# A new order table for a fused attention and two-MoE kernel, and the last four stores on ScalarE's queue

## The chip, the cores and the metric

One core of one Trainium2 chip runs the whole kernel. The metric is the device time of one execution in microseconds (us); lower is better. TensorE (PE) does the matrix products, VectorE (DVE), ScalarE (ACT) and GpSimd (POOL) the work between them, and SyncE (SP) issues nearly all transfers.

## What is computed

Three stages, one after the other. First a gated linear attention over 4 batches, 8 heads, 768 steps and a head size of 48; its result, transposed, is x with 3072 rows and 384 columns. Then a feed-forward layer of width 2048 with a rational function in the middle, and a second one of width 1536 with a gate:

```python
for t in range(S):
    state = alpha[:, :, t, :, None] * state + np.einsum('bhd,bhe->bhde', k[:, :, t], v[:, :, t])
    y[:, :, t] = np.einsum('bhd,bhde->bhe', q[:, :, t], state)
...
h = x @ w_in
P = a[0] + a[1] * h + a[2] * h**2 + a[3] * h**3
Q = 1.0 + np.abs(b[0]) * np.abs(h) + np.abs(b[1]) * h**2
x = (P / (Q + 1e-06)) @ w_out
...
g = x @ w_gate
out = (g * (1.0 / (1.0 + np.exp(-g))) * (x @ w_val)) @ w_out2
```

The weights arrive as 64-bit floats.

## The kernel before, in words

**Precision.** TensorE works on 32-bit numbers rounded to a shorter form, so each operand is kept as a high part and a low part (the rest), and each product is three matmuls: high by high, high by low, low by high (`mm3`, L954 to L957 in moe1; L1209 to L1211 for the last product of moe2). The low part is a subtraction, on GpSimd or on VectorE: `low` (L643, the instruction's line is L645) for weights, `sub` (L923, line L925) for x and for gg, the result of the rational function.

**Attention** (L749). The 3072 steps are cut in 24 chunks of 128. For a chunk, TensorE transposes alpha, k and q (aT, kT, qT, L770), ScalarE copies alpha (al, L779), VectorE runs two scans along the steps, which give running products (bb, L786) and the same backwards (cc, L794), with a reciprocal between them (L790); ScalarE takes the last product of each head (bC, L798). VectorE scales k and q with them (kt L802, qt L812), TensorE makes the scores (sc, L821), which ScalarE copies (aa, L830) and GpSimd masks (L835); then come a transpose back (kn_ps L846, kn L849), the values and the update of the state (upd L865, yT L870 and L876), the state itself (st_c L899, L902, L904; st_s L909) and the store of the chunk's x (L890).

**Weights.** `split_` (from L616) turns a 64-bit tile into high and low parts: a load (L639), two VectorE instructions that cut and join bits (e L669, x L675), and for the first six tiles three more on VectorE (r L683 and L689, x L693), for the others one on ScalarE and one of GpSimd (L697, L702); ScalarE writes the high part (L680, L699) and `low` the low part. The first feed-forward has 16 tiles of w_in (win) and 16 of w_out (wout).

**First feed-forward** (moe1, L959). x comes in six blocks of 512 rows. `load_x` (L929) loads three tiles of a block (xr, L938) and makes their high and low parts (L943, L925). For each of 16 tiles of the width, TensorE makes h (nine matmuls), the three other engines the rational function (t1, t2, t4, L988 to L1010, h L1003 and L1006), and ScalarE and GpSimd the two parts of gg (L1014, L925); TensorE adds gg times wout into three accumulators (acc). At the end of a part the accumulators are evicted (ys, L1039, L1040, L1045) and stored. The blocks are worked on in parts that are interleaved with attention: h of the first tile of block 0 is the first MoE matmul of the program, and block 1's h follows when its x is there.

**Second feed-forward** (moe2, L1150). From about 545 us on nothing but this is left for TensorE: gate and value products, the gate's function, and the last product, which in the last blocks lands with rows on partitions (po, L1209 to L1211). Each of the last block's four row tiles is evicted by ScalarE (L1273) or VectorE (L1274) into os and stored (L1279). In the last block (n == NT // TB - 1) the odd row tiles' stores are issued by ScalarE, the even ones by SyncE; all other stores are SyncE's (L1278).

**What sets the order.** The functions above only enter operations in a plan: `Plan.op` (L250) keeps, for each, its possible forms (engine, cost, function) and what it depends on. `ORDER` (L21), a table of 3746 numbers found by a search, says in which order they are emitted: a number is 2 x operation + choice of form, so that 1325 is operation 662 in its second form. `Plan.order` (L276) walks the table, asserts that what an operation depends on has been emitted, and gives out PSUM banks and weight tiles, first free first. Each engine runs its instructions in the table's order, and semaphores keep the dependencies; a wait on an engine holds up all that is behind it there. For most operations the form is fixed; for `low`, `sub` for x, the step t2 of the rational function (L988 on ScalarE, or GpSimd) and evictions the table chooses the engine. The first forms of `low` are VectorE for the first six weight tiles and GpSimd after them; the last bit of an entry is the choice.

```python
for x in table:
    i, k = x >> 1, x & 1
    _, how, deps, writes, follows = self.ops[i]
    assert i not in done and done.issuperset(deps) and done.issuperset(follows)
```

Of the kernel before, what the change touches and what calls it, by code (L numbers as in the profile page):

```python
# [457 lines left out]
def gla_moe_moe2_kernel(  # L458
# [15 lines left out]
    nc = tc.nc  # L474
    ctx.enter_context(tc.manual_schedule())
    B, H, S, D = q.shape
    NT, DM = out.shape
# [8 lines left out]
    TB = 512  # L486
# [82 lines left out]
    for nm in "akqv":  # L569
        for i in range(NBV if nm == "v" else 1):  # L570
            t = A.tile([128, H, 64], F32, name=f"nat{nm}{i}")
# [760 lines left out]
    t, vs2 = end_a + 5.14, []  # L1332
# [61 lines left out]
```

## Time and profile before

| what | value |
|---|---|
| time, median of 3 runs | 988.67 us (988.14 to 989.16) |
| the profiled execution: its time / its span | 987.1 us / 985.3 us |
| busy, share of the span: TensorE | 969.0 us (98%) |
| VectorE, ScalarE, GpSimd | 80%, 60%, 46% |
| matmuls (PE instructions) | 5355 |
| transfers | 113.51 MB, mean 115 GB/s |

The profiled execution's span is measured on the chip; 1.8 us of its time lie around the span. A matmul record overlaps the next one (512 columns follow each other every 0.23 us and are shown with 0.39), so a busy TensorE is not one at its peak. In rows of a timeline the first number is the start in us, the second the duration in us; "x3" means that three instructions of a kind are joined, and the brackets give the idle time of the engine before it and what ended that. Names as `t<-t,h` are the tiles written and read.

### The profile page before, as it was taken

What the parts mean: (1) busy time and instruction counts of PE and PEld (TensorE: products, weight loads), DVE (VectorE), ACT (ScalarE), POOL (GpSimd) and SP (SyncE); (2) the same over time, 40 slices, a digit from 0 to 9 for tenths busy, and PEclk for the clock granted to TensorE, in tenths of its full rate; (3) what the DMA queues carried; (4) which work ended last, traced back from release to release, by engine and by line L of the source; (5) the groups of instructions that cost most, each with busy time, mean ns of one, the idle gap of its engine ahead of it and who ended that gap; (6) DMA issues with size and microseconds to landing.
All of it is one profiled execution on the core that took longest, in us unless ns stands there. A gap on an engine that the chain in (4) does not pass through costs nothing.

```text
span 985.3 us, 15291 instructions
## 1 busy us (share of the span) xinstructions
PE 969.0 (98%) x5355; PEld 805.6 (82%) x5355; DVE 786.9 (80%) x1493; ACT 588.9 (60%) x1078; POOL 450.5 (46%) x426
## 2 busy tenths in 40 slices
PE   8899999999999999999999999999999999999997
PEld 7777888888888888888888888888888888888886
DVE  7999999999889888888898896799887767733222
ACT  4588998899999787789988675222122222212111
POOL 3368888799877676777987555000000000000000
PEclk9999999999999999999999999999999999999999
DMA  8978666531223242101221663346665545501000
GB/s 184 208 186 220 150 156 152 157 103 37 57 88 94 54 140 70 55 25 53 91 86 45 218 188 127 113 129 196 176 179 187 165 140 150 161 1 33 1 0 34
DMA packets 167137, 113.51 MB, mean 115 GB/s; under 512 B 115472, under 2 KB 140560, under 8 KB 167056
## 3 DMA queue, kind: packets, MB, share of 16 engines
q1 hardware_dynamic: 166768, 112.10, 40.7%
q8 instruction: 43, 0.70, 0.3%
q10 hardware_dynamic: 288, 0.39, 0.1%
q14 instruction: 38, 0.31, 0.1%
HBM read 95.95 MB, written 16.52 MB: 114 GB/s over the span
## 4 chain that ended last, share of the span: by engine, by line
PE 84%; DVE 8%; ACT 4%; issue 2%; POOL 1%; DMA 1%; SPq 0%; DVEq 0%; ACTq 0%; POOLq 0%
PE acc L955 6%; PE acc L956 6%; PE acc L957 6%; PE h L955 5%; PE h L957 5%; PE h L956 5%; PE pg L957 5%; PE pg L955 5%; PE pg L956 5%; PE pv L957 5%; PE pv L955 5%; PE pv L956 5%; PE po L955 4%; PE po L957 4%; PE po L956 4%
## 5 line engine op out<-in xcount | busy, mean ns | idle before, releaser
L925 POOL TENSOR_TENSOR gg<-t,gg 128x512 fp32r<-128x512 f32 x96 | 129.8, 1352 | 52.2 <-ACT gg L1014 50.9
L998 POOL TENSOR_TENSOR t<-t,t 128x512 f32<-128x512 f32 x96 | 127.7, 1332 | 29.2 <-ACT t L988 20.6
L1177 DVE TENSOR_TENSOR sg<-sg,pv 128x512 f32<-128x512 f32 (+1 forms) x73 | 49.4, 678 | 101.3 <-PE pv L957 101.0
L1179 ACT CAST pp<-sg 128x512 fp32r<-128x512 f32 (+1 forms) x73 | 44.8, 615 | 142.1 <-DVE sg L1177 126.7
L1175 ACT ACTIVATE sg<-pg 128x512 f32<-128x512 f32 (+1 forms) x73 | 43.0, 591 | 144.0 <-PE pg L957 143.8
L955 PE MATMUL h<-xt,win 128*128 128x512 f32 x288 | 114.4, 397 | 0.2 <-DVE wo_x L675 0.2
L955 PE MATMUL acc<-gg,wout 128*128 128x512 f32 x288 | 113.9, 396 | 0.5 <-DVE win_x L675 0.5
L957 PE MATMUL h<-xt,win 128*128 128x512 f32 x288 | 112.4, 390 | 0.0
L957 PE MATMUL acc<-gg,wout 128*128 128x512 f32 x288 | 112.3, 390 | 0.0
L956 PE MATMUL acc<-gg,wout 128*128 128x512 f32 x288 | 112.3, 390 | 0.0
L956 PE MATMUL h<-xt,win 128*128 128x512 f32 x288 | 112.2, 390 | 0.0
L957 PE MATMUL pg<-yy,wg 128*128 128x512 f32 x216 | 84.2, 390 | 0.0
L956 PE MATMUL pg<-yy,wg 128*128 128x512 f32 x216 | 84.2, 390 | 0.0
L955 PE MATMUL pg<-yy,wg 128*128 128x512 f32 x216 | 84.1, 389 | 0.0
L957 PE MATMUL pv<-yy,wv 128*128 128x512 f32 x216 | 84.0, 389 | 0.0
L956 PE MATMUL pv<-yy,wv 128*128 128x512 f32 x216 | 84.0, 389 | 0.0
L955 PE MATMUL pv<-yy,wv 128*128 128x512 f32 x216 | 84.0, 389 | 0.0
L1004 DVE SCALAR_TENSOR_TENSOR t<-t,h 128x512 f32<-128x512 f32 x96 | 65.4, 682 | 19.2 <-ACT h L1003 18.7
L995 ACT ACTIVATE t<-h,prm 128x512 f32<-128x512 f32 x96 | 73.8, 775 | 7.1 <-POOL gg L925 6.7
L1102 DVE TENSOR_SCALAR_CACHE_REDUCE chk_x<-chk_e 128x384 f32<-128x384 uint32 x136 | 73.6, 549 | 2.7
L1002 ACT ACTIVATE t<-t,oneps 128x512 f32<-128x512 f32 x96 | 69.5, 724 | 9.3 <-POOL t L998 8.9
L999 DVE TENSOR_TENSOR t<-t,h 128x512 f32<-128x512 f32 x96 | 65.1, 680 | 10.2 <-ACT t L995 10.0
(154 smaller groups left out, 2472.8 us busy)
## 6 DMA issues: line engine op xcount, KB each, us to landing
chk<-in_moe_w_out_dram SPq DMA_DIRECT2D x28, 384.0 KB, 3.2
yr<-y1d SPq DMA_DIRECT2D x36, 256.0 KB, 2.9
xr<-xd SPq DMA_DIRECT2D x27, 256.0 KB, 3.4
y1d<-ys SPq DMA_DIRECT2D x27, 256.0 KB, 3.2
win_st<-in_moe_w_in_dram SPq DMA_DIRECT2D x16, 384.0 KB, 4.1
wout_st<-in_moe_w_out_dram SPq DMA_DIRECT2D x16, 384.0 KB, 3.9
chk<-in_moe_w_in_dram SPq DMA_DIRECT2D x16, 384.0 KB, 3.5
nata<-in_alpha_dram SPq DMA_DIRECT2D x24, 192.0 KB, 3.6
```

The costliest lines, as they stand in the source:

```text
L925: return lambda: eng.tensor_tensor(out_(), in0(), in1().bitcast(F32), ALU.subtract)
L955: nc.tensor.matmul(out_, wh, xh, start=start, stop=False)
L956: nc.tensor.matmul(out_, wh, xl, start=False, stop=False)
L957: nc.tensor.matmul(out_, wl, xh, start=False, stop=stop)
L995: plan.op(v, [act(T, lambda: nc.scalar.activation(t4(), h(), AF.Identity, scale=a3, bias=a2), 2, False)], (hb,), (b4,))
L998: plan.op(v, [pool(T, lambda: nc.gpsimd.tensor_tensor(t1(), t1(), t2(), ALU.mult))], (b1, b2), (b1,))
L999: plan.op(v, [dve(T, lambda: nc.vector.tensor_tensor(t4(), t4(), h(), ALU.mult))], (b4, hb), (b4,))
L1002: plan.op(v, [act(T, lambda: nc.scalar.activation(t2(), t1(), AF.Ln, bias=oneps), 1)], (b1,), (b2,))
L1004: plan.op(v, [dve(T, lambda: nc.vector.scalar_tensor_tensor(t1(), t1(), ONE_EPS, h(), ALU.add, ALU.mult))], (b1, hb), (b1,))
L1102: [(DVE, 0.5, lambda: nc.vector.tensor_scalar(dst(), src(), bound, 0.0, op_, ALU.add, accum_out=cnt.t[:, c : c + 1]))],
L1177: plan.op(v, [(DVE, 0.07 + 0.53 * d, lambda sg=sg, z=z: nc.vector.tensor_tensor(sg.t[:, z], sg.t[:, z], pv.t[:, z], ALU.mult))], (sg, pv), ...
L1179: plan.op(v, [(ACT, 0.1 + 0.43 * d, lambda sg=sg, pp=pp, z=z: nc.scalar.copy(pp.t[:, 0, z], sg.t[:, z]))], (sg,), (pp,))
```

## The change

Three edits. In the table, 2791 of the 3746 entries differ: those from the second to number 2895 (with few exceptions), and four at the end. Operations and their dependencies are the same. On the engines' own sequences, TensorE's 551 operations differ at 221 places, VectorE has 1331 operations instead of 1333, ScalarE 1064 instead of 1076 and GpSimd 423 instead of 409; SyncE's transfers differ at 208 of 377 places. One hundred operations change their engine: 17 weight subtractions go from GpSimd to VectorE and 17 the other way, 28 of t2 from ScalarE to GpSimd and 18 back, 7 subtractions for x from GpSimd to VectorE and 3 back, 5 evictions of the first feed-forward from ScalarE to VectorE and 4 back, and the eviction of the last row tile of the last block from ScalarE to VectorE. The third edit is the queue of the last block's stores: all four on ScalarE's. The diff, cut to lines that the text speaks of (1325 and 1324 are the subtraction for wout0, 1357 and 1356 for wout1, 1974 and 1975 one for x of block 1):

```diff
 ORDER = [
...
-    1332, 294, 254, 298, 160, 162, 214, 256, 266, 1325, 300, 1334, 220, 302, 1344, 1346, 222, 296, 308, 336, 310,
...
-    1771, 1354, 454, 1372, 1357, 1376, 376, 1378, 456, 1382, 274, 1390, 442, 450, 1772, 1800, 412, 378, 324, 416,
...
-    1478, 672, 1473, 1490, 1492, 1946, 712, 1972, 1918, 670, 1922, 1920, 1974, 1482, 714, 1978, 644, 678, 688, 1924,
...
+    266, 308, 216, 264, 268, 224, 226, 310, 306, 336, 338, 1358, 332, 270, 312, 218, 330, 340, 352, 382, 390, 1324,
...
+    406, 446, 400, 448, 402, 1354, 1356, 404, 360, 364, 334, 1760, 1766, 408, 1762, 1768, 58, 1374, 440, 274, 1390,
...
+    1473, 1981, 1975, 718, 1924, 1490, 1492, 720, 1926, 1928, 722, 1982, 678, 688, 1930, 1496, 1984, 1932, 684, 680,
...
-    6732, 6740, 6730, 6748, 6734, 6742, 6736, 6744, 6738, 6746, 6750, 6752, 6755, 6758, 6760, 6763, 6766, 6756, 6764,
+    6732, 6740, 6730, 6748, 6734, 6742, 6736, 6744, 6738, 6746, 6750, 6752, 6755, 6758, 6756, 6760, 6763, 6767, 6764,
     6768,
 ]
...
-            q = nc.scalar if n == NT // TB - 1 and t % 2 else nc.sync
+            q = nc.scalar if n == NT // TB - 1 else nc.sync
             plan.op(vl, [(DMA, 0.6, lambda os=os, r0=r0, q=q: q.dma_start(out[r0 : r0 + 128, :], os.t))], (os,), ())
```

At the end of the table 6755, 6758, 6763 and 6766 or 6767 are the evictions of the four row tiles, and 6756, 6760, 6764 and 6768 their stores.

## Rows read from the trace of the kernel before

**Rows 1.** Windows: us from:to, length, busy of PE, PEld, DVE, ACT, POOL, PEclk, DMA share, GB/s.

```profile
5.66:54.00 48.34, 41.77 (x518) 35.97 (x517) 46.75 (x76) 25.85 (x61) 15.74 (x20) 1.00 0.91 208
54.00:103.00 49.00, 47.62 (x429) 39.58 (x426) 48.48 (x83) 44.22 (x92) 38.61 (x38) 1.00 0.82 200
103.00:545.00 442.00, 441.40 (x2452) 363.79 (x2451) 402.69 (x629) 386.68 (x692) 352.49 (x315) 1.00 0.32 89
545.00:975.00 430.00, 430.00 (x1925) 359.07 (x1924) 286.39 (x703) 128.49 (x230) 40.34 (x37) 1.00 0.41 123
```

**Rows 2.** Waits of TensorE, 54 to 81 us: total us, times, longest.

```profile
PE acc L955 <- DVE win_x L675: 0.5, 1, 0.5
PE kT L770 <- DVE st_c L902: 0.5, 1, 0.5
```

**Rows 3.** Timeline of VectorE, up to the third low half of x.

```profile
19.64 1.23 DVE L786 TENSOR_TENSOR_SCAN bb<-al,seed_f 112x516 f32<-112x516 f32 x1 [0.47 <-ACT bC L798]
...
41.60 0.55 DVE L645 TENSOR_TENSOR win<-win_x,win 128x384 fp32r<-128x384 f32 x1
42.06 0.55 DVE L669 TENSOR_SCALAR win_e<-win_st 128x384 uint32<-128x384 uint32 x1
...
53.10 0.67 DVE L925 TENSOR_TENSOR xt<-xr,xt 128x512 fp32r<-128x512 f32 x1
```

**Rows 4.** Timeline of TensorE: first MoE matmul, and block 1's with the scores before.

```profile
53.99 0.48 PE L955 MATMUL h<-xt,win 128*128 128x512 f32 x1
...
101.93 0.38 PE L821 MATMUL sc<-qt,kt 48*128 48x128 f32 x2
...
103.39 0.48 PE L955 MATMUL h<-xt,win 128*128 128x512 f32 x1
```

**Rows 5.** Timeline of GpSimd: wout1's low half, and an addition at 101.66 us.

```profile
54.32 1.33 POOL L645 TENSOR_TENSOR wout<-wout_x,wout 128x384 fp32r<-128x384 f32 x1 [3.33 <-DVE wout_x L693]
...
101.66 1.35 POOL L702 TENSOR_TENSOR win_x<-win_x,win_r 128x384 uint32<-128x384 uint32 x1
```

**Rows 6.** Timeline of all engines, 72 to 78 us: the second gg's way.

```profile
72.32 1.23 DVE L786 TENSOR_TENSOR_SCAN bb<-al,seed_f 112x516 f32<-112x516 f32 x1
...
73.18 0.62 ACT L1014 CAST gg<-t 128x512 fp32r<-128x512 f32 x1
...
74.61 1.27 POOL L925 TENSOR_TENSOR gg<-t,gg 128x512 fp32r<-128x512 f32 x1
...
75.36 0.68 DVE L999 TENSOR_TENSOR t<-t,h 128x512 f32<-128x512 f32 x1
...
77.69 0.39 PE L955 MATMUL acc<-gg,wout 128*128 128x512 f32 x1
```

**Rows 7.** Timeline of VectorE, 101.4 to 103 us.

```profile
101.43 0.72 DVE L925 TENSOR_TENSOR xt<-xr,xt 128x512 fp32r<-128x512 f32 x1
102.07 2.03 DVE L786 TENSOR_TENSOR_SCAN bb<-al,seed_f 112x516 f32<-112x516 f32 x1
```

**Rows 8.** Groups of VectorE by line, 0 to 103 us: busy us, mean ns | idle.

```profile
L786 DVE TENSOR_TENSOR_SCAN bb<-al,seed_f 112x516 f32<-112x516 f32 x14 | 18.7, 1333 | 6.4 <-ACT al L779 5.7 <-ACT bC L798 0.5
L794 DVE TENSOR_TENSOR_SCAN cc<-al,seed_r 112x516 f32<-112x516 f32 x13 | 16.8, 1289 | 0.1
```

**Rows 9.** Timeline of the end (SPq, ACTq: issues of transfers).

```profile
978.70 0.38 ACTq L1279 DMA_DIRECT2D out_dram<-os  x1
978.71 0.56 DVE L1274 COPY os<-po 128x384 f32<-128x384 f32 x1 [0.23 <-PE po L1211]
...
979.24 0.48 ACT L1273 COPY os<-po 128x384 f32<-128x384 f32 x1 [0.57 <-PE po L1211]
979.75 0.34 ACTq L1279 DMA_DIRECT2D out_dram<-os  x1
```

**Rows 10.** The tile os: from the issue of a store to its landing.

```profile
DMA to landing us min/median/max: 1.9/3.6/3.7
```

**Rows 11.** Line L1361, end of the program: duration ns, first and last start.

```profile
L1361 SPq EVENT_SEMAPHORE  x8: 17/17/17, 983.4 to 983.9; - x8
```

292 rows, old and new, of the table ORDER are left out of this document.

## The prediction, made before the changed kernel was run

> **What bounds the kernel now.** I read the windows by stage first, then TensorE's waits, then the order of single instructions on VectorE, and last the end of the program. The windows [rows 1] show TensorE busy without a gap for the 430 us from 545 to 975, and 441.40 of the 442.00 us before that: there the other engines' order has 0.60 us to give, and no more. What is left stands early. From the first VectorE instruction to 54 us TensorE is busy for 41.77 of 48.34 us, since attention alone can't fill it, and from 54 to 103 us it is idle for 1.38 us, 0.5 of it for a weight split on VectorE and 0.5 for an update of the state, also on VectorE [rows 2]. In the same first stage VectorE itself is busy for 46.75 of 48.34 us. So the kernel is bound by TensorE from about 54 us on, and before that by VectorE, whose order sets when the first MoE matmul can start: that one waits for the third low half of x, at 53.10 on VectorE [rows 3], and starts at 53.99 [rows 4]. After it, every microsecond by which TensorE's work is pushed back lands in the total, but for the idle that it closes up. The new table is therefore priced at three places: the first MoE matmul, the idle after it, and the end. The profiled execution took 987.1 us (span 985.3), 1.57 under the median of 988.67; the sum below is a difference taken in its trace, and I add it to the median.
>
> **The table, up to the first MoE matmul.** In the new table VectorE has three more instructions ahead of that third low half of x, and none fewer: the low halves of wout0 and wout1, which leave GpSimd, and the sum that makes wout1's exact value, which moves up. From one such subtraction to the next instruction the queue takes 42.06 - 41.60 = 0.46 to 0.47 us [rows 3], so 3 x 0.47 = +1.41 us. On GpSimd wout1's subtraction took 1.33 us, but at 54.32 [rows 5], behind the start of the first MoE matmul: where it stood it delayed nothing. Against this stands VectorE's idle time in the stage, 48.34 - 46.75 = 1.59 us, the one wait of which I can name is the 0.47 us before the scan at 19.64, for ScalarE's copy bC [rows 3]. The new table puts that copy three places earlier on ScalarE and a later scan four places later on VectorE, so I take this wait as gone and the rest as staying: +1.41 - 0.47 = +0.94, rounded to **+0.9 us** at 54 us. The ends: +1.41 (nothing regained) and 1.41 - 1.59 = -0.18 (all of it).
>
> **From 54 to 103 us.** A start later by 0.9 gives the engines that feed TensorE 0.9 us more before its waits of 54 to 103 us, 1.38 in all. If all close, the net is 0.9 - 1.4 = -0.5. Two things limit this. First, the second block of the feed-forward: the new table puts six instructions of VectorE that now follow its last vector operation (72.32 to 75.36, 3.04 us [rows 6]) ahead of it, and the two added low halves, and takes one low half away: 3.04 + 0.94 - 0.47 = +3.51. That operation then ends at 72.32 + 3.51 = 75.83, and with ScalarE's copy (0.62) and GpSimd's low half (1.27) its data are there at 77.72; the matmul is at 77.69 now, and two transposes of some 0.44 each go ahead of it, so it is wanted at 78.56 or later. The cover is 0.8 us; without it the whole lateness would be TensorE's. I cost it at nothing. Second, the x of block 1. Ahead of its last low half VectorE gets five instructions (four low halves of weights, and the low half of x that was GpSimd's, 102.07 - 101.43 = 0.64 [rows 7]: 4 x 0.47 + 0.64 = 2.52) and gives up five (three low halves and two bit steps, 5 x 0.47 = 2.35): +0.17, less the 0.47 regained. Its end, 101.43 + 0.72 = 102.15, becomes about 101.85. But the first matmul on this x now starts at 103.39 and the new table takes it ahead of the scores at 101.93 and a transpose [rows 4], 1.46 us earlier in the order. So it finds x ready just about when TensorE gets there: TensorE can be ahead of its present time by 0.1 us at most. I take **-0.1 us** for all that lies before 103 us, in place of the -0.5.
>
> **From 103 us on.** The exchange of engines (17 low halves each way between GpSimd and VectorE, 28 steps of the rational function from ScalarE to GpSimd and 18 back, ten of x, nine evictions, one at the end) is work beside TensorE: in this stage VectorE has 39, ScalarE 55 and GpSimd 90 us of idle [rows 1], which hides it. What it can give is the 0.60 us of TensorE's idle, half of which I take: **-0.3 us**. If the cover fails somewhere, I take the like of today's waits, +0.6. TensorE's own order differs at 221 of 551 places by at most eight, with about as many changes between kinds of work: 0. SP's loads are issued in another order too; nothing in this stage waits for them now, and I cost them at nothing.
>
> **The end.** Now ScalarE evicts the fourth tile at 979.24 and issues its store at 979.75, the last of four [rows 9]. In the new table VectorE evicts it, behind the third (978.71 + 0.56 = 979.27): the copy is through at about 979.83, and ScalarE issues at 979.88, **+0.13 us**. SP has no store left there. ScalarE's queue holds all four: an issue takes it 0.34 to 0.38, so the first goes at 978.70, the second at 979.08 and the third, which waits for VectorE's copy at 979.27, at 979.45; the fourth is behind them and would be free to go at 979.8, before its copy is through. SP's waits at the end begin at 983.4, when the last store has landed [rows 11], so the path is eviction, issue, landing. A landing took 1.9 to 3.7 us [rows 10]. Four stores on one queue, where two lay on each, are in no row: the ends are -0.3 (ScalarE is at once ready for the issue) and +0.6 (a landing longer by a third of its 1.8 us of spread); I take 0, nearest to today's last store, which is on that queue already.
>
> **Sum.** -0.1 - 0.3 + 0.13 = -0.27: 988.67 - 0.27 = **988.4 us**. About 0.2%, 2 us, is what a measurement of this kernel can tell from no change, so the likeliest outcome is that nothing is measured. Its own range is 986.8 to 990.2: at the low end all idle after 54 us closes (1.38 + 0.60, less 0.13), at the high end the first 1.41 stays in full, with the end's 0.13.
>
> **Rivals.** *Faster: the early stage packs.* All of VectorE's 1.59 us comes back, the 1.38 and the 0.60 close, and half of what the scans lose goes too. A scan takes 1.23 us undisturbed [rows 3], and the two kinds 1.333 and 1.289 on average up to 103 us [rows 8]: 14 x 0.10 + 13 x 0.06 = 2.2 us, half of it 1.1. Then 1.41 - 1.59 - 1.38 - 0.60 - 1.1 + 0.13 = -3.1: 985.5 us. For it: a table that differs at 2791 places has the room. Against it: the x of block 1, which must come 3 us earlier too. *Slower: VectorE and GpSimd get into each other's way.* The scan at 102.07 took 2.03 us, while GpSimd ran an addition from 101.66 to 103.01 [rows 5, 7]. If more such pairs meet and the lengthening doubles, block 1's x ends at 102.15 + 0.17 + 2.2 = 104.5, where TensorE wants it at 101.93: +2.6, with the end +2.7, 991.4 us. It decides from the point at which more than about 2 us of lengthening is added before 102 us. *The stores.* They change nothing, or land up to 0.6 us late: 988.4 to 989.0, inside the likeliest case.
>
> The Trainium skill's page "SBUF — State Buffer" (section "SBUF: two separate sides") speaks against such moves: a VectorE instruction with two inputs in SBUF and a GpSimd one that reads it share a port pair under an exclusive lock, and the later waits for the whole of the other. By that rule a scan would be held to GpSimd's end, 103.01, and run 1.23 after it, to 104.24; the trace has it end at 104.10, so it bears the rule out here, and the slower rival above is what it would do.
>
> **How the numbers follow.** No measurable change 0.54, faster 0.30, slower 0.16. The faster case has VectorE's unexplained 1.1 us of idle for it; the slower one needs some three meetings as bad as the one at 102.07 (0.80 us each), among five instructions that VectorE gains before 103 us and five that it loses; 27 scans lose 2.2 us today, 0.08 each. Both ends of the unknown costs lie within 985.6 to 991.0, which cuts off the outer parts of the two rivals.
>
> **What would show it.** The first MoE matmul at 54.9 (wrong if at 53.9 or before), TensorE's idle of 54 to 103 us under 1.38, block 1's first matmul at 101.6 to 102.2, the scans' means still near 1.33 and 1.29, the last store issued 0.1 us later after TensorE's end than now. The prediction is wrong if the first 103 us differ by more than 2 us, or if TensorE is idle after 103 us for more than 1.2 us.

## The result: slower by half a per cent, and the profile after

The changed kernel took 995.0 us (992.25 to 996.05, 4 runs) against 988.77 for the kernel before on the same chip: a ratio of 1.0051 (95% interval 1.0034 to 1.0067). Timed again it came to 1.0032 (1.0013 to 1.0051; experiment 10). It is slower, by 3 to 5 us if the two ratios are taken and by 6.2 and 4.6 us if the medians are; forecast were 988.4 us and a range that ended at 991.0. The profiled execution read here took 992.25, its span 990.4.

The windows of the changed kernel, by the stages of [rows 1] (columns as there):

```profile
5.66:54.00 48.34, 41.37 (x513) 35.75 (x514) 46.60 (x76) 25.36 (x60) 14.25 (x20) 1.00 0.91 205
54.00:103.00 49.00, 46.37 (x402) 37.55 (x404) 48.53 (x80) 42.55 (x87) 35.08 (x35) 1.00 0.77 190
103.00:545.00 442.00, 439.98 (x2464) 361.99 (x2459) 401.36 (x623) 381.11 (x683) 370.25 (x328) 1.00 0.32 89
545.00:975.00 430.00, 429.77 (x1919) 357.97 (x1919) 288.52 (x707) 128.89 (x231) 45.37 (x41) 1.00 0.41 124
```

TensorE's idle is 49.00 - 46.37 = 2.63 us in the second row (1.38 before), 2.02 in the third (0.60) and 0.23 in the fourth (0). Idle shows less than what is lost: a matmul record is 0.39 us long where matmuls start every 0.23, so a start that slips by 0.16 leaves no gap. The lateness of the same operation in the two traces shows all of it. In TensorE's timeline of the changed kernel, the first MoE matmul, an update of the state, block 1's first h and the last matmul:

```profile
54.30 0.48 PE L955 MATMUL h<-xt,win 128*128 128x512 f32 x1
...
72.41 0.61 PE L865 MATMUL upd<-natv,kn 128*64 128x48 f32 x15
...
104.26 0.48 PE L955 MATMUL h<-xt,win 128*128 128x512 f32 x1
...
984.03 0.34 PE L1211 MATMUL po<-wo,pp 128*128 128x384 f32 x1
```

The same update and the last matmul in the kernel before:

```profile
69.58 0.61 PE L865 MATMUL upd<-natv,kn 128*64 128x48 f32 x15
...
978.86 0.34 PE L1211 MATMUL po<-wo,pp 128*128 128x384 f32 x1
```

The first MoE matmul is later by 0.31 us ([rows 4] has 53.99), the update by 2.83, the last matmul by 5.17; the spans differ by 990.4 - 985.3 = 5.1. In between, at places that both orders reach after the same work, TensorE is late by about 2.0 us all the way from 145 to 460 us (a product of acc starts at 443.94 us before and at 445.98 after) and by 5.2 us from 560 us on. So the loss is taken at two places, 54 to 72 us, of which 2.0 us stay, and behind 460 us, where 3.1 us come on top. Windows of 20 and 55 us show the second. First the kernel before, then the changed one:

```profile
440.00:460.00 20.00, 20.00 (x90) 16.34 (x89) 17.23 (x25) 18.63 (x33) 15.66 (x14) 1.00 0.23 76
...
480.00:500.00 20.00, 19.96 (x89) 16.19 (x88) 17.49 (x29) 17.95 (x33) 19.82 (x19) 1.00 0.32 108
...
545.00:600.00 55.00, 55.00 (x245) 45.53 (x244) 46.41 (x76) 38.56 (x78) 31.15 (x28) 1.00 0.59 187
```

```profile
440.00:460.00 20.00, 20.00 (x90) 16.57 (x89) 19.83 (x28) 18.27 (x31) 12.99 (x11) 1.00 0.26 88
...
480.00:500.00 20.00, 18.10 (x77) 13.76 (x76) 18.93 (x32) 17.97 (x32) 15.82 (x14) 1.00 0.30 99
...
545.00:600.00 55.00, 54.77 (x241) 44.76 (x241) 45.70 (x76) 36.67 (x74) 30.03 (x27) 1.00 0.58 190
```

Between 480 and 500 us TensorE starts 77 matmuls instead of 89; at 0.227 us each that is 2.7 us, of which 1.90 shows as idle. Between 545 and 600 it starts 241 instead of 245, 0.9 us. These two counts are the fingerprint that the experiments are read by. The first is the firmer one: a second execution of the changed kernel (e11_after_again) has 77 matmuls again, but 234 in place of 241. TensorE's waits in the changed kernel, 54 to 103 us and then 440 to 600 us (columns as in [rows 2]):

```profile
PE qT L770 <- ACT aa L830: 0.8, 1, 0.8
PE acc L955 <- DVE t L1010: 0.8, 1, 0.8
PE upd L865 <- ACT st_s L909: 0.5, 1, 0.5
PE aT L770 <- ACT aa L830: 0.3, 1, 0.3
...
PE h L955 <- DVE wg_x L675: 1.4, 1, 1.4
PE h L955 <- DVE t L1010: 0.5, 1, 0.5
```

Most of these are no waits for data: the transposes (qT, aT) don't read aa, acc doesn't read t, and h reads neither wg_x nor t. What such a matmul waits for is its place, a PSUM bank, which the named instruction was the last to read: by the rule of `Plan.order`, first free first, qT and aT get the banks of the two sc. (For the wait of upd no such claim is made.) Two of the early ones, on ScalarE and on TensorE:

```profile
67.06 0.35 ACT L909 COPY st_s<-st_c 48x192 f32<-48x192 f32 x1 [1.62 <-POOL st_c L904]
...
67.78 0.56 ACT L830 COPY aa<-sc 128x512 f32<-128x512 f32 x1
...
68.39 0.65 PE L770 MATMUL qT<-ident,natq 128*112 128x128 f32 x4 [0.85 <-ACT aa L830]
...
68.73 0.58 ACT L830 COPY aa<-sc 128x512 f32<-128x512 f32 x1
...
69.37 0.65 PE L770 MATMUL aT<-ident,nata 128*112 128x128 f32 x4 [0.33 <-ACT aa L830]
```

qT starts 68.39 - (67.78 + 0.56) = 0.05 us behind the copy of sc, and aT 0.06 behind the next one. The copies are late by their place in ScalarE's order: the new table has a copy of the state (L909) ahead of them, where ScalarE stands idle for 1.62 us, waiting for GpSimd; the old table has both copies of sc ahead of it. Of the prediction's other marks: the scans' means are 1.309 and 1.319 us (13 of each) against [rows 8], so no sign of a new meeting on VectorE. At the end, the four issues and how long they took to land ([rows 9], [rows 10]):

```profile
983.69 1.86 ACTq L1279 DMA_DIRECT2D out_dram<-os  x4
...
DMA to landing us min/median/max: 2.0/3.4/3.4
```

From the last matmul's start to the span's end it is 990.4 - 984.03 = 6.37 us, against 985.3 - 978.86 = 6.44 before.

### The profile page after: what moved, and what is told of

It reads as the page before. It is cut to its first block, busy times and chain, and to the rows that moved or that the text cites. A ratio compares the mean times of both kernels' runs of the same rounds, so it can differ in the third digit from the quotient of the medians.

```text
span 990.4 us, 15316 instructions
## 1 busy us (share of the span) xinstructions
PE 970.7 (98%) x5355; PEld 804.6 (81%) x5355; DVE 789.0 (80%) x1491; ACT 582.1 (59%) x1066; POOL 468.3 (47%) x440
## 4 chain that ended last, share of the span: by engine, by line
PE 80%; DVE 10%; ACT 4%; POOL 2%; issue 2%; DMA 1%; SPq 0%; DVEq 0%; ACTq 0%; POOLq 0%
PE pv L956 5%; PE pg L956 5%; PE pv L957 5%; PE pv L955 5%; PE pg L957 5%; PE pg L955 5%; PE h L955 5%; PE h L957 4%; PE h L956 4%; PE acc L956 4%; PE acc L955 4%; PE acc L957 4%; PE po L955 4%; PE po L956 4%; PE po L957 4%; PE sc L821 2%
## 5 line engine op out<-in xcount | busy, mean ns | idle before, releaser
L998 POOL TENSOR_TENSOR t<-t,t 128x512 f32<-128x512 f32 x96 | 132.2, 1379 | 17.7 <-ACT t L988 14.5
```

Source lines behind the costliest of these rows:

```text
L998: plan.op(v, [pool(T, lambda: nc.gpsimd.tensor_tensor(t1(), t1(), t2(), ALU.mult))], (b1, b2), (b1,))
```

## The experiments

All kernels here compute the same output; only the table, the engines it chooses and the stores differ. In the diffs of the table, a line holds some neighbouring entries. Five rounds were timed of each.

**1 to 4: which part.** The end alone; the new table for the first 1004 entries only (up to some 190 us); for the rest only; and the new order with the old engines.

```diff
e1_tail, against the kernel before:
-    6758, 6760, 6763, 6766, 6756, 6764,
+    6758, 6756, 6760, 6763, 6767, 6764,
...
-            q = nc.scalar if n == NT // TB - 1 and t % 2 else nc.sync
+            q = nc.scalar if n == NT // TB - 1 else nc.sync
e4_early, against the kernel before (entries 2 to 1084):
-    2, 8, 12, 4, 10,
+    8, 10, 14, 16, 18,
...
e5_late, against the kernel before (entries 1005 to 2895):
-    2360, 2434, 2362, 2426,
+    2360, 2172, 2900, 2362,
...
e2_order, against the changed kernel (103 entries: the choice of engine of 100 operations, and the old end):
-    390, 1324, 1346,
+    390, 1325, 1346,
...
```

> The kernel before with only the end of the change: the last four table entries and all four stores of the last block on ScalarE's queue. Theory A (the table costs the time): 988.5 to 989.0, since in the changed kernel 6.37 us pass from the last matmul's start to the end of the span and in the kernel before 6.44. Rival C (four stores on one queue cost it): 990 or more.

> The new order and its engines for the first 1004 entries (to about 190 us), the old order and engines for what is left, the old end. In the changed kernel's trace TensorE was 2.0 us late at 145 us and 3.2 us more was lost from 470 to 550 us. Theory A (two separate losses): 990.5 to 991.2, and no new loss at 470 to 550 us. Rival B (the early lateness throws the later order out of step): 993.5 to 995.5.

> The old order and engines for the first 1004 entries (to about 190 us), the new ones for what is left, the old end. Theory A (two separate losses): 991.5 to 993, with TensorE waiting for VectorE at 480 to 500 us by 2 us or more. Rival B (the late loss comes from the early lateness): 988 to 989.5.

> The new order for all entries, but each operation on the engine that it had before, and the old end. Theory A1 (the exchange of engines overloads VectorE and GpSimd where both are nearly full): 988.5 to 991. Rival A2 (the order itself costs it, whatever the engines): 993.5 to 995.5.

Measured: the end 989.46 us, ratio 1.0002 (0.9991 to 1.0013); the early part 990.52, 1.0012 (1.0003 to 1.0021); the late part 994.36, 1.0047 (1.0032 to 1.0062); before 989.42. So the end costs nothing, the early part 1.1 us and the late part 4.9. The new order on the old engines took 1050.79, 1.0619 (1.0601 to 1.0637), 61 us that no theory had: order and choice of engine were found together, and the order without its engines is far worse than either kernel. The windows of the early part alone (e4_early), then of the late part alone (e5_late):

```profile
54.00:103.00 49.00, 46.08 (x390) 36.82 (x390) 48.53 (x79) 41.75 (x85) 34.24 (x35) 1.00 0.76 186
...
480.00:500.00 20.00, 19.96 (x89) 16.21 (x88) 17.53 (x30) 18.12 (x33) 19.90 (x20) 1.00 0.31 99
...
545.00:600.00 55.00, 55.00 (x245) 45.54 (x244) 48.23 (x79) 38.57 (x78) 29.25 (x27) 1.00 0.62 193
```

```profile
54.00:103.00 49.00, 47.45 (x435) 39.35 (x436) 48.57 (x84) 42.48 (x88) 35.91 (x38) 1.00 0.85 206
...
480.00:500.00 20.00, 18.29 (x78) 13.98 (x77) 19.21 (x30) 17.32 (x32) 15.88 (x14) 1.00 0.31 99
...
545.00:600.00 55.00, 54.11 (x236) 43.63 (x235) 45.17 (x76) 35.25 (x71) 26.45 (x24) 1.00 0.56 176
```

Each has the fingerprint of its own part: e4_early the idle of 54 to 103 us (2.92) and all 89 and 245 matmuls later on; e5_late the idle of before (1.55), but 78 and 236. The trace of e5_late is of the longest of its six executions (996.27): from 25 to 35 us, where it has the old table, TensorE's granted clock was 0.80 and then 0.52, so its length says nothing of the late part; the windows do.

**5 to 8: three weight halves, one window, t2.** Three of the low halves that leave GpSimd for VectorE lie at 476 to 488 us, just ahead of the waits, two of them drawn out beside a GpSimd instruction (VectorE, then GpSimd, in the changed kernel):

```profile
477.20 1.64 DVE L645 TENSOR_TENSOR wv<-wv_x,wv 128x384 fp32r<-128x384 f32 x1
...
476.95 1.47 POOL L998 TENSOR_TENSOR t<-t,t 128x512 f32<-128x512 f32 x1
```

```diff
e6_after_pool3, against the changed kernel (the three back on GpSimd):
-    4470, 4935, 4949, 4486,
+    4470, 4934, 4948, 4486,
...
-    4960, 4963, 4484,
+    4960, 4962, 4484,
e7_before_dve3, against the kernel before (the three on VectorE):
-    4946, 4934, 4444,
+    4946, 4935, 4444,
...
-    4960, 4948, 4980,
+    4960, 4949, 4980,
...
-    4400, 4962, 4574,
+    4400, 4963, 4574,
e8_window, against the kernel before (the new table at entries 2175 to 2703 alone):
-    4266, 4336, 4268, 4314,
+    4266, 3900, 5436, 5438,
...
e9_after_t2, against the changed kernel (eight t2 steps of 456 to 535 us on their old engines):
-    4432, 4369, 4434, 4328,
+    4432, 4368, 4435, 4328,
...
```

> The changed kernel with three subtractions (the low halves of wg0, wv0 and wo0) back on GpSimd. In the changed trace they start on VectorE at 476.46, 477.20 and 487.13 us and take the queue 0.74, 1.56 and 1.26 us, 3.56 us together, beside TensorE idle of 1.9 us from 480 to 500 us. Theory P (they wait there for GpSimd's instructions, and VectorE is the engine that TensorE waits for): 2 to 3.5 us faster than the changed kernel, 991 to 993. Rival Q (the order of TensorE's and VectorE's work in this stretch costs it, not these three): 994 to 996.

> The kernel before with nothing but the same three subtractions (the low halves of wg0, wv0 and wo0) moved from GpSimd to VectorE. Theory P: slower by 1.5 to 3.5 us, 990.5 to 993, with the three taking 0.7 to 1.6 us each. If only their undisturbed price counts (3 x 0.46 us, beside the idle that VectorE has there): slower by 0 to 0.7. Rival Q: no difference, 988.5 to 989.8.

> The old table but for one window: from entry 2174 (456 us) to entry 2662 (563 us) the new order and the new engines. Theory W (what is lost late is lost in this window alone): 3 to 5 us slower than before, 992 to 994.5. Rival V (the late loss needs the new table from 190 us on): 988.5 to 990.

> The changed kernel with the eight t2 steps of 456 to 535 us that changed between ScalarE and GpSimd back on their old engines (five back to ScalarE, three to GpSimd). Rival G (GpSimd is overloaded by t2 there): 1 us or more faster than the changed kernel, 991 to 994. Theory P (the subtractions on VectorE): within 1 us of the changed kernel, 994 to 996.

Measured, before at 990.12: the three back on GpSimd 994.09, 1.0026 (1.0008 to 1.0044), with 78 matmuls in 480 to 500 us; the three on VectorE in the old table 990.16, 0.9995 (0.9979 to 1.0011). The long low half is real, but neither taking the three away nor putting them in moves the time clear of noise, and without them the late waits stay. The window alone 992.28, 1.0019 (1.0003 to 1.0035): 2.2 us of the loss with the old table on both sides, 82 and 241 matmuls. The eight t2 steps on their old engines 999.47, 1.0084 (1.0059 to 1.0110): the exchange of these eight had been a gain of some 3 to 5 us in this order, and the theory that GpSimd's new share makes the chain late falls.

**9 to 12: the changed kernel again, and scratch in PSUM.** TensorE's largest late wait is for the scratch bank of a weight split (wg_e, then wg_x). Its first instruction was moved right ahead of the last, in both tables; and the old table was put in the window of experiment 7, with the new one around it.

```diff
e10_after_adj, against the changed kernel (23 scratch entries moved):
-    4356, 4952, 4460,
+    4356, 4460,
...
-    4476, 4954,
+    4476, 4952, 4954,
...
e12_before_adj, against the kernel before (54 entries moved the same way)
...
e13_after_nowin, against the changed kernel (the old table at entries 2175 to 2697):
-    4312, 4420, 4294, 4296,
+    4312, 4242, 4272, 4302,
...
```

> The changed kernel, with each weight split from about 435 us on written so that its first VectorE instruction (L669), which takes a PSUM bank as scratch, stands right ahead of the second (L675), which gives the bank back: 23 entries of the table move later. In the changed trace the scratch of wo0 held a bank for 11.6 us and that of wg1 one for 1.9 us, and the first h after them waited 1.6 us for that bank. Theory K (late, TensorE waits for PSUM banks, which the scratch holds): 1.5 to 3.5 us faster than the changed kernel of the same call, 991 to 993.5. Rival D (VectorE's own work is what TensorE waits for; its sum is the same): within 0.7 us of the changed kernel.

> The changed kernel itself once more, as the reference of this call, and for a second trace of it. All theories: 994 to 995.5, slower than before by 4.5 to 6.5 us. If the place of the loss is the table's and not one execution's, the trace shows the waits of 480 to 500 us again.

> The kernel before with the same edit for all its weight splits (54 entries move later), which gives each scratch bank back at once. Theory K: no slower than before, and up to 1 us faster, 987.7 to 989.5, since the kernel before has few such waits (0.2 us at 470.94 us). Rival D: the same as before, 988.5 to 990.

> The changed kernel, with the old order and engines in the window of 456 to 563 us alone. If the late loss is made in this window: 2 to 4 us faster than the changed kernel of the same call, 990.5 to 992.5. If it is made by what the rest of the new table leaves to this window: 993.5 to 995.5.

Measured, before at 989.5: the changed kernel itself (e11_after_again) 994.14, 1.0032 (1.0013 to 1.0051), 12 runs from 992.65 to 995.46; scratch held shorter 996.1, 1.0056 (1.0036 to 1.0076) on the changed table and 1000.28, 1.0084 (1.0052 to 1.0117) on the old one: it costs 2 us, and 8 to 11. Neither theory had that. Theory K isn't settled by it, for the edit lets the scratch begin later and doesn't bring back its bank any sooner. The old table in the window 996.25, 1.0052 (1.0032 to 1.0072), 2 us worse than the changed kernel, not better: 480 to 500 us has its 90 matmuls, and the loss stands in 440 to 480 us (2.13 idle) and 545 to 600 (1.64). Parts of the two tables don't join. In both traces a part of the cost is TensorE's clock; first e10_after_adj, then e13_after_nowin, each a wait and a window (PEclk is the third number from the end) behind it:

```profile
488.16 0.80 PE L955 MATMUL h<-xt,win 128*128 128x512 f32 x1 [2.66 <-DVE wg_x L675]
...
488.00:490.00 2.00, 1.84 (x4) 1.49 (x5) 1.97 (x4) 1.86 (x4) 2.00 (x2) 0.50 0.28 53
```

```profile
464.47 0.50 PE L956 MATMUL h<-xt,win 128*128 128x512 f32 x1 [2.13 <-DVE xt L925]
...
466.00:468.00 2.00, 2.00 (x7) 1.54 (x6) 2.00 (x4) 1.74 (x3) 1.04 (x1) 0.50 0.00 0
```

TensorE stood for 2.66 and 2.13 us, and was then granted 0.50, the lower of its two levels (1.2 GHz): its matmuls start every 0.43 us there instead of 0.23. Behind the 1.43 us of the changed kernel's longest late wait (480 to 500 us) the granted clock is 1.00. So the cost of these two edits is not that of order alone.

The repeat's own profile was its longest, 995.46; its 480 to 500 us is that of the one at 992.25, so the waits there are the kernel's and not an accident of a run:

```profile
480.00:500.00 20.00, 18.07 (x77) 13.78 (x76) 18.97 (x32) 17.30 (x32) 15.82 (x14) 1.00 0.31 99
```

**13 to 16: bank numbers and evictions.** One entry moved, so that the scratch takes another bank; both tables sorted anew by the start times of their own traces, which leaves each engine's sequence as it is and changes only which bank and which weight tile each buffer gets; and three evictions of accumulators moved up.

```diff
k1_after_h5, against the changed kernel:
-    4546, 4482, 4966,
+    4546, 4482, 4574, 4966,
...
-    4536, 4574, 4576,
+    4536, 4576,
k2_after_time, against the changed kernel, and k3_before_time, against the kernel before (entries sorted by start time)
...
k4_after_evict, against the changed kernel:
-    4480, 4502, 4528,
+    4480, 4502, 4400, 4404, 4528,
...
-    4966, 4504, 4968,
+    4966, 4409, 4504, 4968,
...
```

> The changed kernel with one entry moved in the table, so that one buffer gets another PSUM bank (the scratch of wg1 takes bank 7, not bank 0, which the fifth h of the last block is waiting for); every engine's order is the same. Theory K1 (bank numbers alone cost the late loss): 1 to 2 us faster than the changed kernel (993 to 993.5), the wait of 1.6 us at 482.7 us gone. Theory K4 (all banks are held too long): the wait moves to the next h, at 486.6 us, and the time is within 0.6 us of the changed kernel.

> The changed kernel with its table sorted by the start times of its own trace: every engine's order is the same, but banks and weight tiles are given out in the order of time. Theory K1: 2 to 4 us faster than the changed kernel, 990.5 to 992.5. Theory K4 or VectorE's chain: within 1 us of the changed kernel, 993.5 to 995.5.

> The kernel before, with its table sorted by the start times of its own trace in the same way. Theory K1: 0 to 1 us faster than before, as its waits for banks after 100 us are few. Theory K4: within 0.5 us of before.

> The changed kernel with the three evictions of block 4's accumulators moved up, from 485.64, 486.11 (ScalarE) and 490.71 us (VectorE) to where the accumulators are done, about 482.9 us, as in the kernel before (482.1 to 483.8). Theory K4 (the accumulators hold three banks too long): 1 to 2.5 us faster than the changed kernel, 992 to 993.5. Theory K1 or VectorE's chain: within 0.6 us of it.

Measured, before at 989.7: 993.47, 1.0043 (1.0030 to 1.0056); 994.17, 1.0047 (1.0032 to 1.0061); on the old table 990.18, 1.0012 (1.0002 to 1.0021); the evictions 993.65, 1.0047 (1.0032 to 1.0062). No gain clear of noise in any. The first one's 993.47 lies where both of its theories could have it (0.7 us below the changed kernel); its trace decides, on TensorE and on VectorE:

```profile
483.50 0.39 PE L955 MATMUL h<-xt,win 128*128 128x512 f32 x1
...
487.43 0.50 PE L955 MATMUL h<-xt,win 128*128 128x512 f32 x1 [1.73 <-DVE t L1010]
...
486.69 0.68 DVE L1010 SCALAR_TENSOR_TENSOR t<-t,h 128x512 f32<-128x512 f32 x1
```

The h that had waited for the scratch starts at 483.50, without a wait; the next h waits 1.73 us instead, for the bank of an earlier h, whose last reader ends at 486.69 + 0.68 = 487.37. The wait has moved on to the next in line, as theory K4 has it. The new bank numbers of k2_after_time act on the early stage, too: its trace has no wait of acc for L1010 there, but 1.1 and 0.3 us for the two copies of sc and 1.0 us of upd, and 3.15 us of idle in 54 to 103 us. That led to the chain that gives the banks back. The h that starts at 452.10 in both traces, its first reader on ScalarE (L984), and the last reader of its bank (L1010); the kernel before, then the changed one:

```profile
452.10 0.39 PE L955 MATMUL h<-xt,win 128*128 128x512 f32 x1
...
455.55 0.60 ACT L984 ACTIVATE t<-h 128x512 f32<-128x512 f32 x1 [0.48 <-DVE t L1010]
...
467.95 0.69 DVE L1010 SCALAR_TENSOR_TENSOR t<-t,h 128x512 f32<-128x512 f32 x1
```

```profile
452.10 0.39 PE L955 MATMUL h<-xt,win 128*128 128x512 f32 x1
...
462.76 0.58 ACT L984 ACTIVATE t<-h 128x512 f32<-128x512 f32 x1
...
473.35 0.68 DVE L1010 SCALAR_TENSOR_TENSOR t<-t,h 128x512 f32<-128x512 f32 x1
```

TensorE starts this h at the same time only because the new order takes it one place earlier, which makes up for the 2.0 us that TensorE is late. The bank is held 473.35 + 0.68 - 452.10 = 21.9 us instead of 16.5, and the lateness is there from the first reader on: ScalarE's L984 comes 7.2 us later, and from there to the end of L1010 it is 11.3 us instead of 13.1. It can't be this h that holds TensorE up, for its bank, free at 474.03, goes to the h that starts at 474.54 without a wait.

**17 and 18: VectorE relieved.** The finer windows have VectorE at 19.83 of 20 us between 440 and 460 us (17.23 before; 18.59 in e11_after_again): the new table gives it a low half of x there and puts two others earlier. These went back; then the three weight halves of experiment 5 as well.

```diff
k6_relief_early, against the changed kernel (k5_relief_all also has the edit of e6_after_pool3):
-    4178, 5430, 4226,
+    4178, 4226,
...
-    4256, 5436, 4212,
+    4256, 5430, 4212,
...
-    4414, 4417, 4280,
+    4414, 4416, 4280,
...
-    4374, 4376, 4380,
+    4374, 4376, 5436, 4380,
```

> The changed kernel with VectorE given back its old load of 440 to 452 us: the low half of x that the new table gives to VectorE at 451.32 (1.78 us there) is on GpSimd again, and two low halves of the first feed-forward's output, which the new table puts 5 and 13 us earlier on VectorE (443.43 and 450.00), stand about where they were before. Theory V (VectorE is loaded ahead of the last readers of h there, falls 3 to 5 us behind, and hands the PSUM banks on too late at 480 to 500 us): TensorE's idle of 480 to 500 us falls from 1.90 to under 0.7 us, VectorE's busy time of 440 to 460 us from 19.8 to some 17.5 us, and the time to 990.5 to 992.5 us, 2 to 3 below the changed kernel. Rival S (VectorE's lateness there has no such single source; the order and the engines of the whole stage belong together): idle stays over 1.3 us, time 993.3 to 995.5 us.

> The kernel above, and the three weight low halves of 476 to 488 us (the moe2 weights' first three) back on GpSimd, too. Theory V: as above, or up to 0.5 us less, 990.0 to 992.3 us, since the two that run 0.82 and 1.64 us on VectorE at 476.46 and 477.20 leave it just ahead of the waits. Rival S: 993.0 to 995.5 us, with waits of TensorE over 1.3 us in all between 480 and 500 us or moved to a neighbouring stretch.

Measured, before at 989.47: 993.66, 1.0037 (1.0024 to 1.0050), and 993.64, 1.0042 (1.0029 to 1.0055). Rival S has the time of both; the idle of 480 to 500 us, 1.29 and 1.34 us, lies at its limit of 1.3 and is far from theory V's 0.7. The windows of k6_relief_early, and VectorE's two longest waits there, 440 to 500 us:

```profile
440.00:460.00 20.00, 20.00 (x90) 16.57 (x89) 15.07 (x23) 18.12 (x31) 15.28 (x13) 1.00 0.37 114
...
480.00:500.00 20.00, 18.71 (x80) 14.32 (x79) 18.97 (x31) 17.30 (x32) 15.91 (x14) 1.00 0.31 99
...
545.00:600.00 55.00, 54.46 (x237) 43.83 (x236) 45.63 (x77) 35.59 (x73) 26.73 (x25) 1.00 0.57 181
```

```profile
DVE t L1004 <- ACT h L1003: 4.7, 4, 2.7
DVE t L999 <- ACT t L995: 1.8, 3, 0.7
```

VectorE now has 4.93 us of idle between 440 and 460 us, 3.7 and 1.1 of it in these two waits for ScalarE's steps of the same rational function, and TensorE waits on: 80 matmuls instead of 77 in 480 to 500 us, and 237 behind 545 us, between the 241 and the 234 of the changed kernel's two traces. ScalarE's first read of the h followed above is still far behind that h's start: 9.6 us, against 10.7 in the changed kernel and 3.5 before. Relieving VectorE left ScalarE's order as it was, and no run put that order back.

## Why the prediction was wrong

**The failed step is "From 103 us on":** the exchange of engines "is work beside TensorE", hidden by 39 us of VectorE's idle, 55 of ScalarE's and 90 of GpSimd's, with -0.3 us and +0.6 at worst. Measured by itself, from some 190 us on (e5_late), this part costs 4.9 us. Idle time was the wrong cover, for two reasons. It was an average over 442 us, where VectorE has 0.17 us of idle between 440 and 460 in the trace of the changed kernel. And it need not be spare: in k6_relief_early nearly all of VectorE's idle there is waiting inside the chain that hands from engine to engine. The cover that the traces point to is the time until the bank that an h occupies is wanted again, and the trace of before had the time held to read (16.5 us for the h above); no run tested a forecast by it. The step closed with the sentence on TensorE's 221 places, priced at 0 since changes of kind balance; but a changed place also changes which bank an operation takes over, and from whom. At both places of the loss, TensorE's largest waits in the changed kernel are for banks. So were the two waits of [rows 2] that the prediction took for waits for a weight split and for the state: acc doesn't read win_x, nor kT st_c.

**From 54 to 103 us** forecast was -0.1 net of a later start; the trace has the idle at 2.63 instead of 1.38 and the update 2.83 us late. The limits that I had worked out were not the ones that held: neither puts a price on ScalarE's order, nor on a bank. The second block's last vector operation (L1010), forecast to end at 75.83, ended at 77.17 + 0.68 = 77.85, and it did hold TensorE up, but not by its gg:

```profile
74.19 1.28 POOL L925 TENSOR_TENSOR gg<-t,gg 128x512 fp32r<-128x512 f32 x1
...
77.17 0.68 DVE L1010 SCALAR_TENSOR_TENSOR t<-t,h 128x512 f32<-128x512 f32 x1
...
78.00 0.47 PE L955 MATMUL acc<-gg,wout 128*128 128x512 f32 x1 [0.76 <-DVE t L1010]
...
78.58 2.10 POOL L925 TENSOR_TENSOR gg<-t,gg 128x512 fp32r<-128x512 f32 x1 [0.20 <-ACT gg L1014]
```

The first gg was through at 74.19 + 1.28 = 75.47, and its matmul started at 78.00 all the same, 0.15 us behind that L1010: the first accumulator takes the bank of the second block's h. The second gg, feared at 77.72, came at 78.58 + 2.10 = 80.68, and TensorE, late itself, took it at 80.89 without a wait. Block 1's first h, forecast for 101.6 to 102.2, came at 104.26, and TensorE reached it so late by itself: the transpose aT, 99.32 before, stood at 101.82. Both tests that the prediction set itself say wrong: 2.5 us of difference at 103 us (named: 2), and 2.02 + 0.23 us of idle behind it (named: 1.2).

**Up to 54 us** the forecast +0.9 measured +0.31, but not by the path forecast. The third low half of x ended at 55.26 (54.00 + 1.26 with the one beside it) instead of 53.10 + 0.67 = 53.77: +1.49, the +1.41 of the sum with nothing regained. And h started at 54.30 all the same, ahead of that end: the matmul that opens it doesn't read that low half. That it came within 0.6 us of the forecast is luck. The first stage as such is no loss.

**The end** was right: +0.13 forecast, 6.37 - 6.44 = -0.07 in the trace and 1.0002 in e1_tail; four issues on one queue took 1.86 us and the landing 2.0 to 3.4.

**The slower rival** had the sign, but not its mechanism: it put the loss on VectorE and GpSimd drawing each other out before 102 us, and the scans' means say no. Such pairs do occur: the low half at 477.20 takes 1.64 us where one alone takes 0.55 ([rows 3]), and ends at 478.84, 0.42 behind the GpSimd instruction that ends at 478.42. The Trainium skill's page "SBUF — State Buffer" (section "SBUF: two separate sides") says that the later of two such instructions waits for the whole of the other. By its two times this pair agrees. Experiments 5 and 6 show no effect of such pairs on the time that is clear of noise.

**What stays open:** why the banks come back late from some 440 us on. Tried one at a time, the stores, three weight halves, eight t2 steps (their exchange helped), a later start of the scratch, bank numbers, three evictions and VectorE's load of 440 to 452 us give none of the loss back, or no more than the noise hides. The rival left untested is ScalarE's new order, by which the first read of the h above comes 7.2 us later. That the loss has no single source, and lies in how order and engines fit together over the stage, is an inference, not shown by a run. For 54 to 72 us ScalarE's idle ahead of the copies of sc, and the bank waits behind it, are read from the trace; no run put ScalarE's order back there.

## What to carry to other kernels

What the traces suggest, though no run here tested it as a forecast: where a busy engine hands its results through a few buffers to three others, price a reordering by the time that each buffer is held against the time until it is wanted again, stretch by stretch; the other engines' idle, averaged over a stage, hid 4.9 us here. Look at each of the three engines' orders, ScalarE's too: what stands behind a wait there waits with it. Read a wait for something that the instruction doesn't read as a wait for its place, and look for who was late in giving it back; in k1_after_h5, moving the wait to another buffer only moved it. Watch the granted clock when an edit makes TensorE wait longer: 2.1 and 2.7 us of standing were followed by 0.50. And a table that a search found for order and engines together may not come apart: the new order without its engines cost 61 us, and the old table put into a stretch of the new one 2.

## What was not expected

A bank changes hands within 0.05 to 0.06 us of its last reader's end for qT, aT and the h of k1_after_h5, and within 0.15 for acc at 78.00. An idle count understates a loss on TensorE: 1.90 us of idle went with 12 matmuls, 2.7 us. And two executions of the changed kernel, 992.25 and 995.46 us, with the same clock (0.999), lost the same between 480 and 500 us but not elsewhere: TensorE's busy time of 103 to 440 us was 337.00 and 335.56, of 545 to 600 us 54.77 and 53.78.
